# Four more blocks in three matmul passes, and a last chunk that is copied out between its transposes

## The chip, the cores and the metric

The kernel runs on one core of one Trainium2 chip. The metric is the device time of one execution in microseconds. A core has five engines that run their own instruction lists and wait for each other by semaphores: TensorE (PE; its weight loads are shown as PEld), VectorE (DVE), ScalarE (ACT), GpSimd (POOL) and SyncE (SP), which here only issues DMAs. All times in this document are microseconds unless ns is written.

## The reference

Two stages. The first is a polynomial attention with small sketches; the second is a mixture of four dense experts over its output `x` of 4352 tokens by 128 features, and it is where the change lies.

```python
p = domain_probs / (domain_probs.sum(-1, keepdims=True) + 1e-09)
out = np.zeros((N, D))                 # N = 4352, D = 128
for e in range(4):
    h = np.maximum(x @ w1[e], 0.0)     # w1[e]: 128 x 1024
    out += p[:, e:e + 1] * (h @ w2[e]) # w2[e]: 1024 x 128
```

Everything is float32.

## The kernel before

**Chunks and steps.** The 4352 tokens are cut into ten chunks, `CHUNKS = [128, 448, 480 x 7, 416]`, numbered 0 to 9. For each chunk `m` and each expert `e` the 1024 hidden features are eight blocks of 128. A step `i` does two blocks, so an expert takes four steps and a chunk sixteen (`NQ`); a half-step does one block. Tokens lie along the free axis, features on the partitions.

**First product of a block** (`first`, `third`, lines 1141, 1142, 1193): both operands are split beforehand into float32r parts, so that three matmul passes, `xa*wa`, `xb*wb` and `xd*wd`, replace one plain float32 product. Each pass is one instruction. Between the second and the third pass ScalarE scales the PSUM tile (line 1143).

**Second product of a block.** There are two forms. A *plain* block is evacuated by ScalarE into `hid` (line 1207) and multiplied with the float32 weight as one matmul, which the profile shows as two records (`o<-hid,w_sb`). A *three-pass* block is evacuated by ScalarE into `ha` (line 1197); VectorE makes `hb` from it (line 1169, in `lower`), and for each pair of blocks one `hd` (line 1172), or a single one where a block has no partner. Then three passes, `ha*va`, `hb*vb` and `hd*vd`, are issued (line 1274 in `passed`). The first two kinds accumulate in the PSUM tile `o0`, the `hd` passes and the plain products in `o1`.

**Which blocks are three-pass.** `THREE = (0, 1, 3, 4, 5, 6)` always; `OTHER = [2, 7]`. An `(m, e)` in `MORE_IN` also takes block 2, seven of eight; one in `ALL_IN` takes all eight. The extra weights are split while the kernel runs by `more_weight_parts(e, k)` at given steps: two ScalarE and two VectorE instructions of 128 columns per weight, in two parts.

**The order** of second products is written out by hand. A table (`DEAL`, `DEAL_MORE`, `DEAL_ALL`, `DEAL_END`) gives each product a slot, counted in half-steps from the expert's start; `to_due` queues them and `behind` issues those that are due between the first products. In `DEAL_MORE` the last `o1` product has slot 11, in `DEAL_ALL` slot 12 (`d7=12`), and block 7's `hb` product slot 10. `o0` and `o1` have one buffer each; the next expert's first `hd` products come at its slot 6.

**Closing an expert** (`close`, `gather`): after the last `o0` product ScalarE evacuates `o0` into `ev` (line 1277). After the last `o1` product, in chunks 7 to 9, ScalarE copies `o1` into `rest` (line 1358), and GpSimd adds both, multiplies with the gate and adds into `total` (lines 1361, 1368, 1370). In earlier chunks, and for expert 2 of chunk 9, VectorE adds `o1` (line 1355). `ev`, `rest` and `total` have one buffer, the gates two; SyncE reloads a gate when GpSimd is through with the older one.

**The end** (expert 3 of chunk 9, `at_end`): six blocks go in three passes. The last two, 2 and 7, are multiplied with the gate as they are evacuated (line 1203 on VectorE, 1209 on GpSimd) and go through `by_token`, where the tokens are the output's partitions: four products of up to 128 tokens for each block (line 1301) into one PSUM tile `y`, whose four column blocks hold 128, 128, 128 and 32 tokens. `finish` adds `ev`, `o1`, the gate and `total` on VectorE in six operations (lines 1285 to 1287). Four products with an identity (line 1308) then turn that sum and add it into `y`. ScalarE copies columns 0 and 1 to `rows` (line 1313), VectorE columns 2 and 3 (lines 1314, 1315), and four DMAs store one column block each (line 1318), two from SyncE's queue and two from ScalarE's.

Of the kernel before, what the change touches and what calls it, by code (L numbers as in the profile page):

```python
# [9 lines left out]
F32 = mybir.dt.float32  # L10
BF16 = mybir.dt.bfloat16
F32R = mybir.dt.float32r
# [6 lines left out]
def _ap(t, p0: int, np_: int, off: int, free):  # L19

    p = list(t.ap)[0]
    return bass.AP(t.tensor, t.offset + p0 * p[0] + off, [[p[0], np_]] + [list(d) for d in free])
# [3 lines left out]
def kernel(  # L26
# [24 lines left out]
    nc = tc.nc  # L51

    P = 128
    HP = 64
    B, H, S, D = q.shape
    E, DM, F = w1.shape
    R = 8
    R2 = 2 * R
    G = S // 32
# [6 lines left out]
    CW = 480  # L66
# [4 lines left out]
    OTHER = [b for b in range(FB) if b not in THREE]  # L71
# [18 lines left out]
        a0=4, b0=4, a1=4, b1=5, a2=5, a3=5, d0=6, d1=6, b2=6, a4=7, b3=7, a5=8, b4=8, d2=9, d3=9,  # L90
        b5=9, d4=10, d5=10, x6=11, x7=11,
    )
    ALL_IN = {(7, 2), (8, 2), (9, 2)}
    UNITS = [[P, 448, 512], [576, 512], [576, 512], [576, 512]]

    SPLITS = [
# [7 lines left out]

    CHUNKS = [P, 448] + [480] * 7 + [416]
    NC = len(CHUNKS)
    MORE_IN = {(2, 2), (3, 2), (4, 2), (5, 0), (5, 2), (5, 3), (6, 2), (7, 0), (7, 1), (7, 2), (7, 3), (8, 0), (8, 1), (8, 2), (8, 3), (9, 0), (9, 1), (9, 2)}
    MORE_AT = {0: (73, 75), 1: (56, 57), 2: (38, 39), 3: (77, 78)}
    START = [sum(CHUNKS[:m]) for m in range(NC)]
    assert all(sum(u) == S for u in UNITS) and sum(CHUNKS) == B * S  # L110
# [3 lines left out]
    apool = ctx.enter_context(tc.tile_pool(name="attn", bufs=1))  # L114
    mpool = ctx.enter_context(tc.tile_pool(name="moe", bufs=2))
# [5 lines left out]
    def psum(pool, tag):  # L121
        return pool.tile([P, 512], F32, tag=tag, name=tag)
# [63 lines left out]
    def more(m, e):  # L186
        return (m, e) in MORE_IN

    def three_of(m, e):
        return tuple(range(N3)) if at_end(m, e) else tuple(range(FB)) if (m, e) in ALL_IN else MORE if more(m, e) else THREE  # L190

    def deal_of(m, e):
        return DEAL_END if at_end(m, e) else DEAL_ALL if (m, e) in ALL_IN else DEAL_MORE if more(m, e) else DEAL

    def last_of(m, e, o):
        deal = deal_of(m, e)
        return max((p for p in deal if p[0] in ("ab" if o == 0 else "d" if at_end(m, e) else "dx")), key=lambda p: (deal[p], list(deal).index(p)))
# [4 lines left out]
    def second_weight(e, b):  # L202

        at = split_at(b)
        return w2_of[e, 0 if in_three(b) else 1][:, DM * at : DM * (at + 1)]
# [170 lines left out]
    def parts(m):  # L376

        c, end, at = START[m], START[m] + CHUNKS[m], 0
        while c < end:
            n = min(end, (c // S + 1) * S) - c  # L380
            yield c // S, c % S, n, at
            c, at = c + n, at + n
# [510 lines left out]
    def split(a, w, scale):  # L893
        nc.scalar.activation(a, w, ACTF.Copy, scale=scale * NEAR)

    def join(out, in0, scale, in1, op):
        nc.vector.scalar_tensor_tensor(out=out, in0=in0, scalar=scale, in1=in1, op0=ALU.mult, op1=op)
# [47 lines left out]
    def more_weight_parts(e, k=OTHER[0]):  # L945

        w = second_weight(e, k)
        if k != OTHER[0]:
            abd = apool.tile([P, 3 * P], F32R, tag="fs", name="vm")
            a, b, d = (abd[:, P * i : P * i + P] for i in range(3))  # L950
        elif e % 2 == 0:
            if "sr" not in more_home:
                more_home["sr"] = cpool.tile([P, 6 * P], F32R, tag="sr", name="vm")
            a, b, d = (more_home["sr"][:, P * i : P * i + P] for i in range(3 * (e // 2), 3 * (e // 2) + 3))
        else:
            ab = apool.tile([P, 2 * P], F32R, tag="kvz", bufs=2, name="vm")
            a, b = ab[:, 0:P], ab[:, P : 2 * P]
            d = (apool if e == 1 else cpool).tile([P, P], F32R, tag="rd" if e == 1 else "sq", name="vm")[:, :]
        split(a, w, 4096.0)
        join(b, w, 4096.0, a.bitcast(F32), ALU.subtract)  # L960
        yield
        split(a, w, 1.0)
        join(d, b.bitcast(F32), 1.0, a.bitcast(F32), ALU.subtract)
        w2_parts[e][k] = a, b, d
        yield
# [107 lines left out]
    def at_end(m, e):  # L1073
        return (m, e) == (NC - 1, E - 1)

    def block_of(m, e, k):
        return (THREE + tuple(OTHER))[k] if at_end(m, e) else k
# [180 lines left out]
    begun_o, evs = set(), {}  # L1258

    def passed(m, e, what, k, hd):  # L1260

        n, o = CHUNKS[m], 0 if what in "ab" else 1
        if what == "x" and at_end(m, e):
            return by_token(m, e, k, hd)
        if (m, e) not in acc:
            acc[m, e] = [None, None]
        if acc[m, e][o] is None:
            acc[m, e][o] = psum(ps_o, f"o{o}")
        first_one = (m, e, o) not in begun_o
        begun_o.add((m, e, o))  # L1270
        last = last_of(m, e, o) == what + str(k)
        b = block_of(m, e, k)
        w, h = (second_weight(e, b), hd) if what == "x" else (w2_parts[e][b]["abd".index(what)], hd["abd".index(what)])
        nc.tensor.matmul(acc[m, e][o][:, 0:n], w, h, start=first_one, stop=last)  # L1274
        if last and o == 0:
            evs[m, e] = mpool.tile([P, CW], F32, tag="ev", bufs=1, name="ev")
            nc.scalar.activation(evs[m, e][:, 0:n], acc[m, e][0][:, 0:n], ACTF.Copy, scale=1.0 + R12)
        if last and o == 1:
            finish(m, e) if at_end(m, e) else close(m, e)

    def finish(m, e):

        n, o1, ev, g = CHUNKS[m], acc.pop((m, e))[1], evs.pop((m, e)), gate.pop((m, e))
        for x in (slice(0, 2 * P), slice(2 * P, n)):
            nc.vector.tensor_tensor(out=ev[:, x], in0=ev[:, x], in1=o1[:, x], op=ALU.add)
            nc.vector.tensor_tensor(out=ev[:, x], in0=ev[:, x], in1=g[:, x], op=ALU.mult)
            nc.vector.tensor_tensor(out=ev[:, x], in0=ev[:, x], in1=total[m][:, x], op=ALU.add)
        last_sum[0] = ev
# [3 lines left out]
    def by_token(m, e, k, hd):  # L1292

        n = CHUNKS[m]
        if last_rows[0] is None:
            last_rows[0] = psum(ps_h, "h")
            last_rows.append(lpool.tile([P, 4 * P], F32, tag="kn", name="rows"))
        y, rows = last_rows
        cols = [(c, min(P, n - c)) for c in range(0, n, P)]
        for c, w in cols:  # L1300
            nc.tensor.matmul(  # L1301
                y[0:w, c : c + P], hd[:, c : c + w], second_weight(e, block_of(m, e, k)),
                start=(k == N3 and c == 0), stop=False, skip_group_check=True,
            )
        if k < FB - 1:
            return
        for c, w in cols:
            nc.tensor.matmul(
                y[0:w, c : c + P], last_sum[0][:, c : c + w], eye[0][:, :],
                start=False, stop=True, skip_group_check=True,  # L1310
            )
        ((b, at, _, _),) = parts(m)
        nc.scalar.copy(rows[:, 0 : 2 * P], y[:, 0 : 2 * P])
        nc.vector.tensor_copy(rows[:, 2 * P : 3 * P], y[:, 2 * P : 3 * P])
        nc.vector.tensor_copy(rows[0 : n - 3 * P, 3 * P :], y[0 : n - 3 * P, 3 * P :])
        for queue, c in ((nc.sync, 0), (nc.scalar, 2), (nc.sync, 1), (nc.scalar, 3)):
            c, w = cols[c]
            queue.dma_start(
                bass.AP(out.tensor, out.offset + (b * S + (at + c) // 32) * DM, [[DM, w // 32], [G * DM, 32], [1, DM]]),
                rows[0:w, c : c + P],  # L1320
            )

    eye = [None]
# [63 lines left out]
    def at_step(step, *calls):  # L1387
        to_part.setdefault(step, []).extend(calls)

    def next_of(parts_of):  # L1390
        return lambda: next(parts_of, None)
# [3 lines left out]
    for e, at in zip((2, 3, 0, 1), W2_AT):  # L1395
        parts_of = second_weight_parts(e)
        for hs in at:
            at_half.setdefault(hs, []).append(next_of(parts_of))
    for e, at in MORE_AT.items():
        parts_of = more_weight_parts(e)  # L1400
        for step in at:
            at_step(step, next_of(parts_of))
    parts_of = more_weight_parts(2, OTHER[1])
    for step in (113, 115):
        at_step(step, next_of(parts_of))
    for m in range(2, NC):
        tokens = token_parts(m)
        for step in (NQ * m - 4, NQ * m - 3):
# [6 lines left out]
    def close(m, e):  # L1415

        nonlocal ending
        ended = gather(m, e)
        next(ended)
        ending = chain(ending, ended)  # L1420
        closed[0] = m, e
# [38 lines left out]
    for i in range(len(steps) + LA):  # L1460
# [4 lines left out]
        if i < len(steps):  # L1465
            m, kq = steps[i]
# [72 lines left out]
```

## Time and profile before

| | us |
|---|---|
| median of 3 runs (lowest, highest) | 447.35 (447.32, 447.63) |
| the profiled execution's own time | 447.11 |
| its span, first to last instruction | 445.1 |
| TensorE busy | 437.4 (98%) |
| VectorE busy | 386.5 (87%) |
| ScalarE busy | 345.4 (78%) |
| GpSimd busy | 166.7 (37%) |

The profile is of one execution. A row of the timeline reads: start, duration, engine, line, operation, output and inputs by the program's names, shape, count, and in brackets the engine's idle time before it with what ended it. Matmul durations overlap, because they are pipelined. A row of a grouped view reads: count, busy us and mean ns, then idle time before the group. L1274 is line 1274 of the kernel before.

### The profile page before, as it was taken

To read this page: it belongs to the slowest core of one execution; us is meant where nothing else is said; L and a number is where in the kernel's file an instruction comes from. 1 tells how busy PE (TensorE), PEld (TensorE's weight loads), DVE (VectorE), ACT (ScalarE), POOL (GpSimd) and SP (SyncE) were. 2 spreads that over 40 slices of the span, in tenths; PEclk is the share of its full clock that TensorE was granted. 3 is DMA by queue.
4 is the path that set the end of the run, shared out by engine and by line. 5 is a ranking of instruction groups with operands and counts; after the bars stand their busy time and mean duration, and the time that the engine had idled before them with its cause. 6 is when DMAs were issued, how large, how long until landed. Compare 5 with 4: busy or idle time off the path is not lost.

```text
span 445.1 us, 8123 instructions
## 1 busy us (share of the span) xinstructions
PE 437.4 (98%) x2770; PEld 359.6 (81%) x2770; DVE 386.5 (87%) x616; ACT 345.4 (78%) x721; POOL 166.7 (37%) x243
## 2 busy tenths in 40 slices
PE   9999999999999999999999999999999999999994
PEld 6887678888887887778887888787888888889992
DVE  5998979978999789989997898889988998899893
ACT  4478898848888688868884888687888888888881
POOL 6358523212142023213351354133335463555451
PEclk9999999999999999999999999999999999999998
DMA  7945375224602430235114511260420012002100
GB/s 224 307 114 170 86 174 112 73 56 122 149 24 45 123 90 24 74 83 143 24 28 74 143 19 41 50 159 21 71 50 21 18 46 45 23 13 43 26 20 21
DMA packets 45525, 35.02 MB, mean 79 GB/s; under 512 B 21708, under 2 KB 40268, under 8 KB 45484
## 3 DMA queue, kind: packets, MB, share of 16 engines
q1 hardware_dynamic: 43960, 33.30, 30.0%
q0 software_dynamic: 1184, 1.05, 1.0%
q8 instruction: 22, 0.36, 0.3%
q10 hardware_dynamic: 340, 0.15, 0.2%
q14 instruction: 19, 0.16, 0.1%
HBM read 29.27 MB, written 5.21 MB: 77 GB/s over the span
## 4 chain that ended last, share of the span: by engine, by line
PE 92%; DMA 3%; DVE 1%; SPq 1%; ACT 1%; issue 1%; POOL 0%; DVEq 0%; ACTq 0%
PE o L1274 40%; PE h L1141 14%; PE h L1142 14%; PE h L1193 14%; PE h L272 6%; PE o L1253 3%; DMA w_sb<-in_moe_w_dram 2%; PE h L459 1%; PE o L272 1%; DMA dp<-in_moe_domain_probs_dram 1%; PE h L1301 1%; DVE hb L1169 0%; ACT h L1143 0%; SPq L178 0%; DMA s_raw<-in_S_dram 0%
## 5 line engine op out<-in xcount | busy, mean ns | idle before, releaser
L1143 ACT ACTIVATE h<-h 128x480 f32<-128x480 f32 (+2 forms) x288 | 158.9, 552 | 63.8 <-PE h L1142 56.5
L1169 DVE SCALAR_TENSOR_TENSOR hb<-h,ha 128x480 fp32r<-128x480 f32 (+2 forms) x225 | 140.5, 639 | 28.2 <-ACT ha L1197 25.8
L1172 DVE SCALAR_TENSOR_TENSOR hd<-ha,hb 128x960 fp32r<-128x960 f32 (+4 forms) x120 | 137.9, 1149 | 11.6 <-DVE hb L1169 0.5
L1141 PE MATMUL h<-xa,wa 128*128 128x480 f32 (+2 forms) x288 | 129.5, 450 | 0.0
L1197 ACT ACTIVATE ha<-h 128x480 fp32r<-128x480 f32 (+2 forms) x225 | 126.3, 561 | 0.1
L1193 PE MATMUL h<-xd,wd 128*128 128x480 f32 (+2 forms) x288 | 108.7, 377 | 0.1
L1142 PE MATMUL h<-xb,wb 128*128 128x480 f32 (+2 forms) x288 | 108.0, 375 | 0.0
L1368 POOL TENSOR_TENSOR ev<-ev,gate 128x256 f32<-128x256 f32 (+3 forms) x52 | 46.8, 900 | 146.1 <-DVE ev L1355 138.4
L1274 PE MATMUL o<-ha,vab 128*128 128x480 f32 (+2 forms) x204 | 76.7, 377 | 0.0
L1141 PEld LDWEIGHTS h<-xa,wa 128*128 128x128 f32 x288 | 54.2, 188 | 18.0 <-issue 11.4
L1142 PEld LDWEIGHTS h<-xb,wb 128*128 128x128 f32 x288 | 54.2, 188 | 17.5 <-issue 11.7
L1274 PE MATMUL o<-hd,vd 128*128 128x480 f32 (+2 forms) x204 | 63.7, 379 | 0.2 <-DVE hd L1172 0.2
L1193 PEld LDWEIGHTS h<-xd,wd 128*128 128x128 f32 x288 | 54.0, 188 | 8.9 <-ACT h L1143 0.8
L1370 POOL TENSOR_TENSOR total<-total,ev 128x256 f32<-128x256 f32 (+3 forms) x52 | 55.7, 1072 | 4.1
L1274 PE MATMUL o<-hb,vb 128*128 128x480 f32 (+2 forms) x136 | 51.2, 376 | 0.0
L1274 PE MATMUL o<-hid,w_sb 128*128 128x480 f32 (+2 forms) x90 | 43.2, 561 | 0.0
L1274 PEld LDWEIGHTS o<-hd,vd 128*128 128x128 f32 x204 | 37.8, 188 | 6.3 <-issue 0.8
L1274 PEld LDWEIGHTS o<-ha,vab 128*128 128x128 f32 x204 | 38.3, 188 | 5.1
L1361 POOL TENSOR_TENSOR ev<-ev,rest 128x256 f32<-128x256 f32 (+2 forms) x24 | 16.9, 726 | 63.3 <-ACT rest L1358 63.3
L1207 ACT ACTIVATE hid<-h 128x480 f32<-128x480 f32 (+2 forms) x62 | 34.7, 560 | 1.5 <-PE h L1193 1.4
L1368 POOL TENSOR_TENSOR total<-ev,gate 128x256 f32<-128x256 f32 (+3 forms) x18 | 15.8, 898 | 38.4 <-issue 23.0
L1274 PEld LDWEIGHTS o<-hb,vb 128*128 128x128 f32 x136 | 25.5, 188 | 4.0 <-DVE hb L1169 0.4
(166 smaller groups left out, 466.8 us busy)
## 6 DMA issues: line engine op xcount, KB each, us to landing
gate<-gates SPq DMA_DIRECT2D x16, 240.0 KB, 3.4
kn<-in_k_dram SPq DMA_DIRECT2D x4, 544.0 KB
vn<-in_v_dram SPq DMA_DIRECT2D x16, 128.0 KB, 5.9
qp<-qd SPq DMA_DIRECT2D x8, 256.0 KB
qp<-qd SPq DMA_DIRECT2D x6, 288.0 KB, 4.7
qb<-qd SPq DMA_DIRECT2D x6, 288.0 KB
qn<-in_q_dram SPq DMA_DIRECT2D x3, 544.0 KB
w_sb<-in_moe_w_dram SPq DMA_DIRECT2D x3, 512.0 KB
```

What stands on the lines that cost most here:

```text
L272: nc.tensor.matmul(out(s), weights(s), moving(s), **flags)
L1141: nc.tensor.matmul(g, wa[:, e, w], xa, start=True, stop=False)
L1142: nc.tensor.matmul(g, wb[:, e, w], xb, start=False, stop=True)
L1143: nc.scalar.activation(g, g, ACTF.Copy, scale=1.0 + R12)
L1169: nc.vector.scalar_tensor_tensor(out=hb, in0=g, scalar=0.0, in1=high, op0=ALU.max, op1=ALU.subtract)
L1172: nc.vector.scalar_tensor_tensor(out=d2, in0=a2.bitcast(F32), scalar=R12, in1=b2.bitcast(F32), op0=ALU.mult, op1=ALU.subtract)
L1193: nc.tensor.matmul(g, w, x, start=False, stop=True, skip_group_check=True)
L1197: nc.scalar.activation(ha, g, ACTF.Relu, scale=NEAR)
L1207: nc.scalar.activation(hid[i][j], g, ACTF.Relu)
L1274: nc.tensor.matmul(acc[m, e][o][:, 0:n], w, h, start=first_one, stop=last)
L1368: nc.gpsimd.tensor_tensor(out=to[:, x], in0=ev[:, x], in1=g[:, x], op=ALU.mult)
L1370: nc.gpsimd.tensor_tensor(out=total[m][:, x], in0=total[m][:, x], in1=ev[:, x], op=ALU.add)
```

## The change

Two things are edited.

1. *Second products.* Expert 1 of chunks 7, 8 and 9 moves from seven to eight three-pass blocks, and expert 0 of chunk 6 from six to seven. The weight of block 7 of expert 1 is therefore split too, at steps 114 and 115, into a tile that takes the place of `y` of the attention stage. The second half of the split of expert 2's block 7 moves from step 115 to step 117.
2. *The end.* The last expert's `o0` is evacuated into the buffer of `rest` instead of `ev`. The copies from PSUM are issued between the transposing products instead of behind them all, and the four stores take 32 partitions of all column blocks each, instead of all partitions of one column block. Run `g` of a partition group goes to every fourth output row group (`[4 * DM, t]`).

```diff
-    ALL_IN = {(7, 2), (8, 2), (9, 2)}
+    ALL_IN = {(7, 1), (7, 2), (8, 1), (8, 2), (9, 1), (9, 2)}
...
-    MORE_IN = {..., (5, 3), (6, 2), (7, 0), ...}
+    MORE_IN = {..., (5, 3), (6, 0), (6, 2), (7, 0), ...}
...  # more_weight_parts
-            abd = apool.tile([P, 3 * P], F32R, tag="fs", name="vm")
+            abd = apool.tile([P, 3 * P], F32R, tag="fs" if e == 2 else "y", name="vm")
...  # passed
-            evs[m, e] = mpool.tile([P, CW], F32, tag="ev", bufs=1, name="ev")
+            tag = "rest" if at_end(m, e) else "ev"
+            evs[m, e] = mpool.tile([P, CW], F32, tag=tag, bufs=1, name=tag)
             nc.scalar.activation(evs[m, e][:, 0:n], acc[m, e][0][:, 0:n], ACTF.Copy, scale=1.0 + R12)
...  # by_token
-        for c, w in cols:
+        ((b, at, _, _),) = parts(m)
+        for i, (c, w) in enumerate(cols):
             nc.tensor.matmul(
                 y[0:w, c : c + P], last_sum[0][:, c : c + w], eye[0][:, :],
                 start=False, stop=True, skip_group_check=True,
             )
-        ((b, at, _, _),) = parts(m)
-        nc.scalar.copy(rows[:, 0 : 2 * P], y[:, 0 : 2 * P])
-        nc.vector.tensor_copy(rows[:, 2 * P : 3 * P], y[:, 2 * P : 3 * P])
-        nc.vector.tensor_copy(rows[0 : n - 3 * P, 3 * P :], y[0 : n - 3 * P, 3 * P :])
-        for queue, c in ((nc.sync, 0), (nc.scalar, 2), (nc.sync, 1), (nc.scalar, 3)):
-            c, w = cols[c]
-            queue.dma_start(
-                bass.AP(out.tensor, out.offset + (b * S + (at + c) // 32) * DM, [[DM, w // 32], [G * DM, 32], [1, DM]]),
-                rows[0:w, c : c + P],
+            if i == 1:
+                nc.scalar.copy(rows[:, 0 : 2 * P], y[:, 0 : 2 * P])
+            elif i > 1:
+                nc.vector.tensor_copy(rows[0:w, c : c + P], y[0:w, c : c + P])
+        for g in range(4):
+            t = len([w for _, w in cols if w > 32 * g])
+            (nc.scalar if g % 2 else nc.sync).dma_start(
+                bass.AP(out.tensor, out.offset + (b * S + at // 32 + g) * DM, [[G * DM, 32], [4 * DM, t], [1, DM]]),
+                _ap(rows, 32 * g, 32, 0, [[P, t], [1, DM]]),
             )
...
-    parts_of = more_weight_parts(2, OTHER[1])
-    for step in (113, 115):
-        at_step(step, next_of(parts_of))
+    for e, at in ((2, (113, 117)), (1, (114, 115))):
+        parts_of = more_weight_parts(e, OTHER[1])
+        for step in at:
+            at_step(step, next_of(parts_of))
```

More of the change, by code (lines that the diff above doesn't have):

```diff
@@ L106 @@
     NC = len(CHUNKS)
-    MORE_IN = {(2, 2), (3, 2), (4, 2), (5, 0), (5, 2), (5, 3), (6, 2), (7, 0), (7, 1), (7, 2), (7, 3), (8, 0), (8, 1), (8, 2), (8, 3), (9, 0), (9, 1), (9, 2)}
+    MORE_IN = {(2, 2), (3, 2), (4, 2), (5, 0), (5, 2), (5, 3), (6, 0), (6, 2), (7, 0), (7, 1), (7, 2), (7, 3), (8, 0), (8, 1), (8, 2), (8, 3), (9, 0), (9, 1), (9, 2)}
     MORE_AT = {0: (73, 75), 1: (56, 57), 2: (38, 39), 3: (77, 78)}
```

## The prediction

> **What bounds the kernel now.** I read the page first, its span and its chain that ended last:
>
> ```profile
> span 445.1 us, 8123 instructions
> ...
> PE o L1274 40%; PE h L1141 14%; PE h L1142 14%; PE h L1193 14%; PE h L272 6%; PE o L1253 3%; DMA w_sb<-in_moe_w_dram 2%; PE h L459 1%; PE o L272 1%; DMA dp<-in_moe_domain_probs_dram 1%; PE h L1301 1%; DVE hb L1169 0%; ACT h L1143 0%; SPq L178 0%; DMA s_raw<-in_S_dram 0%
> ```
>
> The chain is TensorE's matmuls, first products and second products. The kernel is bound by the number of matmul passes, so taking passes away shortens it wherever TensorE does not come to wait. The profiled execution took 447.11 us, 2.0 more than its span, and the median of the runs is 447.35. I sum changes against the span of 445.1 and carry the difference over to the median unchanged.
>
> Next, the timeline of TensorE in the last fifth, at one plain second product (`hid,w_sb`):
>
> ```profile
> 304.19 0.97 PE L1274 MATMUL o<-hid,w_sb 128*128 128x480 f32 x2
> ...
> 305.22 0.38 PE L1142 MATMUL h<-xb,wb 128*128 128x480 f32 x1
> 305.44 0.38 PE L1193 MATMUL h<-xd,wd 128*128 128x480 f32 x1
> ```
>
> Durations overlap here, so starts must be read. One pass follows the other after 0.22 (305.22 to 305.44). Between 304.19 and 305.22 lie the plain product and one L1141 pass: 1.03 less 0.22 is 0.81 for the plain product. Three passes take 3 x 0.22 = 0.66. A converted block should thus give TensorE 0.15.
>
> Then whole experts, by windows from one expert's first `ha,vab` pass to the next one's (the columns are the window's length, and busy time with count of PE, PEld, DVE, ACT, POOL):
>
> ```profile
> 271.15:281.92 10.77, 10.77 (x48) 8.64 (x46) 9.39 (x14) 8.67 (x18) 4.17 (x4) 1.00 0.11 29
> 328.29:338.91 10.62, 10.62 (x49) 8.84 (x47) 8.67 (x12) 9.15 (x19) 3.62 (x4) 1.00 0.13 27
> 338.91:349.41 10.50, 10.50 (x50) 8.93 (x48) 9.52 (x13) 9.21 (x20) 5.84 (x6) 1.00 0.10 23
> 370.64:381.26 10.62, 10.62 (x48) 8.83 (x47) 8.68 (x12) 9.15 (x19) 3.61 (x4) 1.00 0.12 31
> 381.26:391.72 10.46, 10.46 (x50) 8.94 (x49) 9.47 (x13) 9.16 (x20) 5.84 (x6) 1.00 0.09 25
> 411.16:420.38 9.22, 9.22 (x49) 8.82 (x49) 7.79 (x12) 8.18 (x19) 3.19 (x4) 1.00 0.17 38
> 420.38:429.49 9.11, 9.11 (x49) 8.92 (x48) 8.26 (x13) 7.91 (x19) 5.17 (x6) 1.00 0.11 23
> ```
>
> The first row is expert 0 of chunk 6, with six blocks in three passes. Then come expert 1 (seven blocks) and expert 2 (all eight) of chunks 7, 8 and 9, in pairs. So the trace already holds the change for the neighbouring expert: all eight instead of seven is worth 0.12, 0.16 and 0.11. The granted clock is 1.00 in every row.
>
> **The second products.** Removed: four plain products, in (6,0), (7,1), (8,1), (9,1). Added: twelve passes. By the windows (7,1) and (8,1) give 0.12 and 0.16; (6,0), six to seven blocks at the same width, gives the 0.15 of the pass count. (9,1) would give 0.11, but I count it as nothing, for a reason in the next rows. Sum: 0.43 off TensorE.
>
> The price is on VectorE: ScalarE trades one activation for another, while each converted block adds a `hb` and half of a paired `hd`.
>
> ```profile
> L1169 DVE SCALAR_TENSOR_TENSOR hb<-h,ha 128x480 fp32r<-128x480 f32 x185 | 117.5, 649 | 22.3 <-ACT ha L1197 20.1 <-PE h L1142 1.9
> L1172 DVE SCALAR_TENSOR_TENSOR hd<-ha,hb 128x960 fp32r<-128x960 f32 x86 | 105.8, 1230 | 8.0 <-DVE hb L1169 0.5
> ...
> L1172 DVE SCALAR_TENSOR_TENSOR hd<-ha,hb 128x480 fp32r<-128x480 f32 x13 | 9.5, 730 | 1.7 <-PE h L1193 0.5
> ```
>
> For an ALL expert a single `hd` becomes a pair: 0.65 + (1.23 - 0.73) = 1.15 per block at most. In (6,0) it is 0.65 + 0.73, as a new single. Does VectorE have that room? Its timeline in expert 1 of chunk 7, the idle time in brackets:
>
> ```profile
> 335.88 0.66 DVE L1169 SCALAR_TENSOR_TENSOR hb<-h,ha 128x480 fp32r<-128x480 f32 x1 [0.55 <-PE h L1142]
> 336.96 0.66 DVE L1169 SCALAR_TENSOR_TENSOR hb<-h,ha 128x480 fp32r<-128x480 f32 x1 [0.42 <-ACT ha L1197]
> ...
> 340.02 0.66 DVE L1169 SCALAR_TENSOR_TENSOR hb<-h,ha 128x480 fp32r<-128x480 f32 x1 [0.57 <-ACT ha L1197]
> ```
>
> The new work falls just ahead of 335.88, and 0.55 + 0.42 + 0.57 = 1.54 of idle time follows before the busy expert 2 begins: 1.15 fits, with 0.39 left. What would be late next is a low product in expert 2, and that has room of its own:
>
> ```profile
> 344.54 1.22 DVE L1169 SCALAR_TENSOR_TENSOR hb<-h,ha 128x480 fp32r<-128x480 f32 x2
> ```
> ```profile
> 346.96 0.38 PE L1274 MATMUL o<-hb,vm 128*128 128x480 f32 x1
> ```
>
> Block 7's `hb` is done at 345.76 and used at 346.96, 1.20 later, so VectorE may lag by that much before TensorE waits. I price the cover at nothing lost; if it is gone, see the second rival. In chunk 9 it is different:
>
> ```profile
> 417.81 0.59 DVE L1169 SCALAR_TENSOR_TENSOR hb<-h,ha 128x416 fp32r<-128x416 f32 x1 [0.24 <-ACT ha L1197]
> 418.75 0.59 DVE L1169 SCALAR_TENSOR_TENSOR hb<-h,ha 128x416 fp32r<-128x416 f32 x1 [0.34 <-ACT ha L1197]
> ...
> 421.40 0.59 DVE L1169 SCALAR_TENSOR_TENSOR hb<-h,ha 128x416 fp32r<-128x416 f32 x1 [0.43 <-ACT ha L1197]
> ```
>
> Here the idle time is 1.01, about what the block adds (1.15 scaled by 416/480 is 1.00). After 421.40 VectorE shows no further idle time until 435.69, and TensorE's last second product waits for it (434.77, below). The tail belongs to VectorE, so TensorE's 0.11 in (9,1) is not passed on.
>
> The split of the weight (1,7) adds two ScalarE and two VectorE instructions at steps 114 and 115, 128 wide, each under the 0.73 of the 480-wide row; they and the second half of (2,7), moved from step 115 to 117, lie inside chunk 7's first expert and well before the use. The tile moves into the attention's `y`, free once its four DMAs have landed; nothing later writes it. A closing that comes one half-step later (last low product in slot 12 instead of 11) starts GpSimd's additions, and behind them SyncE's gate reload, later by an eighth of an expert, 1.3. GpSimd is busy 5.84 of 10.50 at the most in the windows, so I price this at nothing.
>
> **The end.** Its rows, from the timeline:
>
> ```profile
> 434.77 0.65 PE L1274 MATMUL o<-hd,vd 128*128 128x416 f32 x2 [0.19 <-DVE hd L1172]
> 435.13 0.52 ACT L1277 ACTIVATE ev<-o 128x416 f32<-128x416 f32 x1 [0.57 <-POOL total L1370]
> 435.27 2.47 PE L1301 MATMUL h<-w_sb,hid 128*128 128x128 f32 x16
> 435.69 0.42 DVE L1285 TENSOR_TENSOR ev<-ev,o 128x256 f32<-128x256 f32 x1 [0.47 <-ACT ev L1277]
> ...
> 437.67 1.27 PE L1308 MATMUL h<-eye,ev 128*128 128x128 f32 x8
> 438.98 0.37 ACT L1313 COPY rows<-h 128x256 f32<-128x256 f32 x1 [3.33 <-PE h L1308]
> 439.38 0.62 SPq L1318 DMA_DIRECT2D out_dram<-rows  x1
> 439.39 0.29 DVE L1314 COPY rows<-h 128x128 f32<-128x128 f32 x1 [1.42 <-ACT rows L1313]
> ...
> 439.71 0.66 ACTq L1318 DMA_DIRECT2D out_dram<-rows  x1
> ```
>
> `rest` instead of `ev`: ScalarE no longer waits 0.57 for GpSimd, and VectorE's six operations start some 0.2 earlier. That is worth nothing, because TensorE goes from 435.27 to 438.94 without a break.
>
> The copies between the matmuls: L1314 waited for L1313 although the two touch other columns, so two engines take turns at this one PSUM tile. In the changed program's order the third transposing product waits for ScalarE's copy, the fourth for VectorE's. The eight L1308 records take 1.27; the first four, columns 0 and 1, are through at about 438.38 (estimate: half of 1.27 and a little of the overlap). From there, with hand-overs of 0.04 as at 438.94 to 438.98: ScalarE's copy until 438.79, the third product (two records, about 0.45) until 439.3, VectorE's copy 0.29 until 439.62, the fourth product until 440.1, its copy until 440.45. All four DMAs wait for the whole of `rows` now, since each takes 32 partitions of every column block. The first issues fall at 440.48 instead of 439.38: 1.1 late. If the products did not wait, all would be ready about 439.2; that is the other bound.
>
> The DMAs themselves, from the views by line and of DMA issues:
>
> ```profile
> L1318 ACTq DMA_DIRECT2D out_dram<-rows x2: 462/561/660, 439.7 to 440.5; - x2
> DMA to landing us min/median/max: 3.5/3.5/3.5
> ```
> ```profile
> xd<-y SPq DMA_DIRECT2D x22, 64.0 KB, 1.7
> ...
> out_dram<-ob SPq DMA_DIRECT2D x16, 60.0 KB, 2.1
> ```
>
> The last one, 16 KB, is issued at 440.5 and lands 3.5 later, at 444.0; the span ends 1.1 after that. The new form (32 partitions, up to four runs of 512 bytes each) is the form of `xd<-y`, of the same 64 KB, which lands after 1.7; the other stores into the output, also of 32 partitions, take 2.1. The bounds are 1.7 and 3.5. I take 1.9, between the two like forms. The second issue of each queue follows the first by an issue time of 0.4 to 0.66, at about 441.0; landing at 442.9 instead of 444.0 takes 1.1 off the end, in spite of the later start.
>
> Sum: 0.43 + 1.1 = 1.53. Span 443.6, profiled execution 445.6, median 447.35 - 1.53 = 445.8.
>
> **The rivals.**
>
> *The new stores land no sooner.* For it: all are issued at once on two queues, and 3.5 is what this place shows. Against it: both rows of like form. Then the last landing is 441.0 + 3.5 = 444.5, 0.5 later; with 0.43 gained the result is about 447.4, no change. [...]
>
> *VectorE becomes the bound, slower than before.* The mechanism: idle time behind a wait for ScalarE is not room if the wait recurs after the inserted work. Then VectorE enters expert 2 by 1.15 late, and expert 2, where it is busy 9.5 of 10.5, adds to that. It decides from the point where the lag at block 7's `hb` passes 1.20; from there TensorE stops for the excess. With all 1.15 in excess in three chunks and 1.38 in (6,0) that is 4.8, less the 1.53: 450.6. Against it: the 1.54 of idle time, and that ScalarE's own arrivals do not move.
>
> *The products do not wait for the copies.* The stores start at about 439.2, 1.2 earlier than I say: 444.6. Against it stands the 1.42 wait.
>
> **How the numbers follow.** A change of 0.2%, 0.9 us, is about what a measurement of this kernel can tell from none. My forecast, 445.8, gets 0.74, of which 0.05 end with less than 0.9 gained (a landing past 2.5). The first rival, 447.4, gets 0.13; the second 0.08, mostly partial, a 0.01 of it within 0.2%; the third 0.05. Faster: 0.69 + 0.05 = 0.74. Same: 0.05 + 0.13 + 0.01 = 0.19. Slower: 0.07. The range takes the forecast's own (445.2, with landing after 1.7, the shortest issue, (9,1)'s 0.11 and a copy chain 0.2 shorter, to 446.8) and reaches to the first rival: 445.2 to 447.4.
>
> **What would show it.** Right: 41 plain second products instead of 45 at L1274; windows of 10.5 for expert 1 of chunks 7 and 8, with VectorE busy 9.5; ScalarE's last evacuation without its wait; the copies of the end alternating with the transposing products, first store issue near 440.5 less 0.4, and its landing under 2.1. Wrong: VectorE named as releaser of L1274 passes in chunks 7 to 9; stores landing after 3.5; or copies running beside the products.

## The result, and the profile after

| | before | after |
|---|---|---|
| median (lowest, highest), 6 runs each | 447.35 (447.32, 447.63) | 445.47 (445.19, 445.93) |
| the profiled execution's own time, its span | 447.11, 445.1 | 445.93, 443.9 |

The ratio is 0.9957, with a 95% interval of 0.9946 to 0.9969: 1.88 less, where 1.55 less was predicted. The gain is small, 0.4%, but the interval stays clear of 1. The profiled execution of after is the slowest of its six, so its span says less than its parts. The head of the page:

```profile
span 443.9 us, 8142 instructions
...
PE 437.3 (99%) x2774; PEld 360.1 (81%) x2774; DVE 391.5 (88%) x623; ACT 345.4 (78%) x723; POOL 169.6 (38%) x243
```

VectorE was busy 5.0 longer (386.5 before). TensorE did not stop for it in the four experts that changed. Their windows in after, each from its first `ha,vab` pass to the next expert's (columns as in the prediction):

```profile
272.03:282.64 10.61, 10.61 (x48) 8.82 (x47) 10.27 (x15) 8.65 (x17) 3.97 (x4) 1.00 0.11 26
329.01:339.46 10.45, 10.45 (x49) 9.01 (x48) 9.71 (x13) 9.06 (x20) 3.67 (x4) 1.00 0.14 29
...
371.18:381.65 10.47, 10.47 (x49) 9.01 (x48) 9.28 (x12) 8.89 (x19) 3.60 (x4) 1.00 0.12 31
...
411.59:420.68 9.09, 9.09 (x49) 8.90 (x49) 8.25 (x13) 7.91 (x19) 3.20 (x4) 1.00 0.17 38
```

The four are 10.61, 10.45, 10.47 and 9.09 long, against 10.77, 10.62, 10.62 and 9.22 before: 0.16, 0.17, 0.15 and 0.13 less, 0.61 together. That gain cannot be seen in the span, because this execution started late. The first row is of the timeline of before, the others of after:

```profile
28.11 0.47 PE L1141 MATMUL h<-xa,wa 128*128 128x448 f32 x1
```
```profile
20.76 0.77 PE L272 MATMUL h<-x_first,w_sb 128*64 128x128 f32 x8 [0.59 <-DMA w_sb<-in_moe_w_dram]
...
28.94 0.47 PE L1141 MATMUL h<-xa,wa 128*128 128x448 f32 x1
```

The first pass of the wide chunks is 0.83 late, mostly for a weight that had not landed (a wait of 0.59 that before does not have). The first by-token pass, at 435.58, is only 0.31 later than the 435.27 of before. Matched pass by pass, the lateness falls at just the four edited experts, from 0.88 to 0.31. A second profile of the changed kernel (run e_again) has its first wide pass at 28.32 and a span of 443.2, so the 0.83 is of one execution. Now the end in after:

```profile
434.93 0.52 ACT L1278 ACTIVATE rest<-o 128x416 f32<-128x416 f32 x1
...
435.58 2.47 PE L1302 MATMUL h<-w_sb,hid 128*128 128x128 f32 x16
...
437.98 0.71 PE L1310 MATMUL h<-eye,rest 128*128 128x128 f32 x4
438.73 0.37 ACT L1315 COPY rows<-h 128x256 f32<-128x256 f32 x1 [3.28 <-PE h L1310]
...
439.15 0.49 PE L1310 MATMUL h<-eye,rest 128*128 128x128 f32 x2 [0.46 <-ACT rows L1315]
439.68 0.29 DVE L1317 COPY rows<-h 128x128 f32<-128x128 f32 x1 [1.41 <-PE h L1310]
440.00 0.84 ACTq L1320 DMA_DIRECT2D out_dram<-rows  x2
...
440.02 0.41 PE L1310 MATMUL h<-eye,rest 128*32 128x128 f32 x2 [0.38 <-DVE rows L1317]
440.47 0.28 DVE L1317 COPY rows<-h 32x128 f32<-32x128 f32 x1 [0.50 <-PE h L1310]
440.81 0.82 SPq L1320 DMA_DIRECT2D out_dram<-rows  x2
```
```profile
L1320 SPq DMA_DIRECT2D out_dram<-rows x2: 337/384/432, 440.8 to 441.2; - x2
...
DMA to landing us min/median/max: 1.7/1.7/1.7
```

Product and copy alternate, each with the other named as its releaser: the staircase of the prediction. ScalarE's queue issues at 440.00, after the third block's copy, because its two stores need three column blocks only; SyncE's first store needs the fourth, and its second stands behind it. The last store, issued at 441.2, lands 1.7 later (3.5 before). From the first by-token pass to the span's end it is 443.9 - 435.58 = 8.3, before 445.1 - 435.27 = 9.8: the end gained 1.5.

What the stores do while in flight is in two stretches of each trace, the DMA engines' busy share and GB/s being the last columns (before, then after):

```profile
440.64:441.54 0.90, 0.00 (x0) 0.00 (x0) 0.00 (x0) 0.00 (x0) 0.00 (x0) 1.00 0.26 67
441.54:443.44 1.90, 0.00 (x0) 0.00 (x0) 0.00 (x0) 0.00 (x0) 0.00 (x0) 0.81 0.31 80
```
```profile
440.87:441.74 0.87, 0.00 (x0) 0.00 (x0) 0.00 (x0) 0.00 (x0) 0.00 (x0) 1.00 0.49 124
441.66:442.54 0.88, 0.00 (x0) 0.00 (x0) 0.00 (x0) 0.00 (x0) 0.00 (x0) 1.00 0.54 133
```

The old stores hold the share at 0.26 to 0.31 of 16 engines, which is four or five engines' worth, for 2.8; the new ones reach 0.5 and are through in two bursts of 0.9.

### The profile page after: what moved, and what is told of

Same layout as the page of the kernel before. It is cut to its first block, busy times and chain, and to the rows that moved or that the text cites. A ratio compares the mean times of both kernels' runs of the same rounds, so it can differ in the third digit from the quotient of the medians.

```text
span 443.9 us, 8142 instructions
## 1 busy us (share of the span) xinstructions
PE 437.3 (99%) x2774; PEld 360.1 (81%) x2774; DVE 391.5 (88%) x623; ACT 345.4 (78%) x723; POOL 169.6 (38%) x243
## 4 chain that ended last, share of the span: by engine, by line
PE 94%; DMA 3%; SPq 1%; DVE 1%; issue 0%; ACT 0%; POOL 0%; ACTq 0%
PE o L1274 41%; PE h L1193 14%; PE h L1141 14%; PE h L1142 14%; PE h L272 6%; PE o L1253 3%; DMA w_sb<-in_moe_w_dram 2%; PE h L459 1%; PE o L272 1%; SPq L178 1%; DMA dp<-in_moe_domain_probs_dram 1%; PE h L1302 1%; SPq L165 0%; DMA s_raw<-in_S_dram 0%; PE h L1310 0%
## 5 line engine op out<-in xcount | busy, mean ns | idle before, releaser
L1169 DVE SCALAR_TENSOR_TENSOR hb<-h,ha 128x480 fp32r<-128x480 f32 (+2 forms) x229 | 142.6, 638 | 22.4 <-ACT ha L1197 21.0
L1172 DVE SCALAR_TENSOR_TENSOR hd<-ha,hb 128x960 fp32r<-128x960 f32 (+3 forms) x121 | 140.7, 1163 | 11.7 <-DVE hb L1169 0.5
L1197 ACT ACTIVATE ha<-h 128x480 fp32r<-128x480 f32 (+2 forms) x229 | 128.5, 561 | 0.1
L1141 PE MATMUL h<-xa,wa 128*128 128x480 f32 (+2 forms) x288 | 128.0, 444 | 0.0
L1193 PE MATMUL h<-xd,wd 128*128 128x480 f32 (+2 forms) x288 | 108.8, 378 | 0.1
L1193 PEld LDWEIGHTS h<-xd,wd 128*128 128x128 f32 x288 | 54.1, 188 | 9.1 <-ACT h L1143 0.8
L1363 POOL TENSOR_TENSOR ev<-ev,rest 128x256 f32<-128x256 f32 (+2 forms) x24 | 19.4, 830 | 61.7 <-ACT rest L1360 61.7
L1274 PE MATMUL o<-hid,w_sb 128*128 128x480 f32 (+2 forms) x82 | 39.4, 562 | 0.0
L1207 ACT ACTIVATE hid<-h 128x480 f32<-128x480 f32 (+2 forms) x58 | 32.5, 561 | 1.5 <-PE h L1193 1.4
```

Source lines behind the costliest of these rows:

```text
L1141: nc.tensor.matmul(g, wa[:, e, w], xa, start=True, stop=False)
L1169: nc.vector.scalar_tensor_tensor(out=hb, in0=g, scalar=0.0, in1=high, op0=ALU.max, op1=ALU.subtract)
L1172: nc.vector.scalar_tensor_tensor(out=d2, in0=a2.bitcast(F32), scalar=R12, in1=b2.bitcast(F32), op0=ALU.mult, op1=ALU.subtract)
L1193: nc.tensor.matmul(g, w, x, start=False, stop=True, skip_group_check=True)
L1197: nc.scalar.activation(ha, g, ACTF.Relu, scale=NEAR)
L1207: nc.scalar.activation(hid[i][j], g, ACTF.Relu)
```

## The experiments

Runs sent together share a chip and the runs of the kernel before; each ratio is to those. At the end of this section a table sets the end of all kernels side by side.

**The two halves, each alone.** `e_second` is the kernel before with the `ALL_IN`, `MORE_IN`, `tag` and step edits; `e_end` is the kernel before with the edits in `passed` (`rest`) and `by_token`.

> The kernel before with the second products of the change alone; the end of the program stays as it was. Theory (TensorE passes): the traces show the four experts 0.12 to 0.17 shorter each, 0.57 together, so the time is 446.8 (447.35 - 0.55), with 41 plain products, and from the first by-token pass to the span's end still 9.8. Rival (the gain lies in the end alone, and the profiled run's late start of 0.83 hides a body that gained nothing): 447.3. Rival of VectorE (it becomes the bound): above 447.4.

> The kernel before with the end of the change alone: the tile of the last evacuation, the copies between the transposing products, the stores by 32 partitions. Theory: the end, counted from the first by-token pass to the span's end, is 8.3 instead of 9.8, so the time is 445.85 (447.35 - 1.5). The prediction had 446.25 (1.1 less). Rival (part of the 1.5 comes from the body): 446.3 or more.

Measured: `e_second` 446.65, ratio 0.9982 (0.9974 to 0.9991); `e_end` 445.8, ratio 0.9969 (0.9958 to 0.9981); before 447.46. In the traces the halves do not mix: the first by-token pass is at 434.67 in `e_second` (0.60 sooner than before) and at 435.24 in `e_end` (0.03 sooner), and from there the ends take 444.4 - 434.67 = 9.7 and 443.5 - 435.24 = 8.3. The rows of the first and then of the second:

```profile
span 444.4 us, 8140 instructions
```
```profile
434.67 2.47 PE L1301 MATMUL h<-w_sb,hid 128*128 128x128 f32 x16
```
```profile
span 443.5 us, 8125 instructions
```
```profile
435.24 2.47 PE L1302 MATMUL h<-w_sb,hid 128*128 128x128 f32 x16
```

So the second products give 0.6 and the end 1.5. The rival that the body (all that comes before the first by-token pass) gained nothing falls.

**Copies or stores?** `e_old_copies` is the changed kernel with all copies behind the products:

```diff
-            if i == 1:
-                nc.scalar.copy(rows[:, 0 : 2 * P], y[:, 0 : 2 * P])
-            elif i > 1:
-                nc.vector.tensor_copy(rows[0:w, c : c + P], y[0:w, c : c + P])
+        nc.scalar.copy(rows[:, 0 : 2 * P], y[:, 0 : 2 * P])
+        nc.vector.tensor_copy(rows[:, 2 * P : 3 * P], y[:, 2 * P : 3 * P])
+        nc.vector.tensor_copy(rows[0 : n - 3 * P, 3 * P :], y[0 : n - 3 * P, 3 * P :])
```

> The changed kernel with the three copies put back behind all four transposing products; stores of the new form. Theory (the stores' form is the whole gain, the new order of the copies costs time): the data is ready 4.6 after the first by-token pass instead of 5.2, and the last landing comes 0.6 sooner: end of 7.7, time 444.9. Rival (the order of the copies is a part of the gain): 446 or more, slower than the changed kernel's 445.47.

`e_old_stores` is the changed kernel with the old loop over `(nc.sync, 0), (nc.scalar, 2), (nc.sync, 1), (nc.scalar, 3)` in place of the loop over `g`.

> The changed kernel with the four old stores, by column block of up to 128 partitions; the copies stay between the products. Theory (stores' form): each store lands 3.5 after its issue; the last, of the fourth block, is issued about 5.2 after the first by-token pass and lands at 8.7 or later: end of 9.8, no better than before; time 446.8, the second products' gain alone. Rival (the gain is the order of the copies, or the earlier first stores): end of 8.3, 445.5.

Measured: `e_old_copies` 445.16, ratio 0.9949 (0.9937 to 0.9962); `e_old_stores` 445.86, ratio 0.9964 (0.9952 to 0.9976). The first has an end of 442.7 - 434.89 = 7.8, which is 0.45 shorter than with copies between the products (8.26 in e_again): by the traces the new order of the copies costs time, as predicted, and the stores' form earns more than the whole gain of the end. The medians of the two, 445.16 and 445.47, are too close to show it. The second was a miss: its end is 443.9 - 434.75 = 9.15, not 9.8. Its rows:

```profile
434.75 2.47 PE L1302 MATMUL h<-w_sb,hid 128*128 128x128 f32 x16
...
438.30 1.26 SPq L1320 DMA_DIRECT2D out_dram<-rows  x2
```
```profile
L1320 ACTq DMA_DIRECT2D out_dram<-rows x2: 517/589/661, 439.2 to 439.9; - x2
...
DMA to landing us min/median/max: 2.8/2.8/2.8
```

The last old store landed 2.8 after its issue, not 3.5. But 439.9 + 2.8 = 442.7 is 4.4 after the first issue at 438.30. In before that distance was 439.38 to 444.0, 4.6. The 3.5 was not the price of one store; the four together take some 4.5 from the first issue on. The early copy of blocks 0 and 1 therefore helps the old stores (first issue 3.55 after the first by-token pass instead of 4.1).

**Is it so?** `e_banks_old_stores` gives the by-token sums three PSUM tiles (below), which makes all data ready earlier but leaves the first issue where it is. The stores are the old ones.

> Three PSUM tiles as in the run before, with the old stores by column block. Theory (the old stores are held to a rate of their own: in three traces the last landing came 4.3 to 4.6 after the FIRST issue, whenever the last was issued): the first store leaves when it did with one tile, 3.55 after the first by-token pass, so the last landing is at 7.9 to 8.1 although all data is ready 1.1 sooner; end of 9.1, 0.8 over the changed kernel's 8.3, 0.8 slower than the changed kernel beside it. Rival (each old store lands some 3 after its own issue): last issue 4.5, landing 7.4, end of 8.5, like the changed kernel.

Measured 446.33, ratio 0.9977 (0.9969 to 0.9986); the changed kernel beside it 445.29.

```profile
L1321 SPq DMA_DIRECT2D out_dram<-rows x2: 575/599/623, 438.3 to 439.0; - x2
L1321 ACTq DMA_DIRECT2D out_dram<-rows x2: 639/644/650, 438.4 to 439.2; - x2
...
DMA to landing us min/median/max: 3.6/3.6/3.6
```

With the first by-token pass at 434.74, the last issue moved from 5.2 to 4.45 after it and the landing did not move (8.0). So the last store does not land at a fixed time after its own issue. The end of 9.4 is longer than the 9.1 expected: 1.4 instead of 1.1 lie behind the landing, and why stays open.

**Why are the old stores held to that rate?** `e_swapped` is `e_old_stores` with two dimensions of the destination exchanged, so that rows of the result lie in other places:

```diff
-                bass.AP(out.tensor, ..., [[DM, w // 32], [G * DM, 32], [1, DM]]),
+                bass.AP(out.tensor, ..., [[G * DM, 32], [DM, w // 32], [1, DM]]),
```

> The stores by column block of the kernel before (128 partitions each), with the two outer dimensions of the destination exchanged: 32 rows of one stride outside, 4 inside. Bytes, runs of 512 and the set of addresses are the same, but rows of the result change places. The copies are those of the changed kernel. Theory (what sped the stores up is the destination's outermost dimension, 32 instead of 4, over how many DMA engines the transfer is spread): the last store lands 1.7 to 2.1 after its issue at 5.2 past the first by-token pass, the end is 8.0 to 8.4, the time 444.7 to 445.1. Rival (what counts is 32 partitions instead of 128 for one transfer): as with the old stores, end of 9.15, time 445.9.

Measured 444.76, ratio 0.9939 (0.9926 to 0.9951).

```profile
L1320 ACTq DMA_DIRECT2D out_dram<-rows x2: 524/592/661, 439.3 to 440.0; - x2
...
DMA to landing us min/median/max: 1.6/1.6/1.6
```
```profile
439.65:440.65 1.00, 0.04 (x1) 0.00 (x0) 0.28 (x1) 0.00 (x0) 0.00 (x0) 1.00 0.48 143
```

Partitions, bytes, queues and issues are those of `e_old_stores`; the landing falls from 2.8 to 1.6 and the DMA share rises to 0.48 (0.29 to 0.32 in `e_old_stores`). What counts here is the destination's outer dimension, 32 or (for the three stores of 128 tokens) 4, not how many partitions a store takes. The exchanged form also writes four neighbouring rows in turn, but that is not needed: the rows of the new form are `4 * DM` apart, and its last store lands after 1.7. The share fits the theory that the outer dimension sets over how many DMA engines a store is spread: 0.29 to 0.32 is some five of the 16 engines' worth, and the exchanged form's 0.48 in the first 1.00 and 0.39 in the next 0.62 are six to eight. Which engines a single store takes, and by what rule, no run shows.

**Why do product and copy take turns?** `e_banks`:

```diff
-            last_rows[0] = psum(ps_h, "h")
+            last_rows[0] = [psum(ps_h, "h") for _ in range(3)]
...
+        of = {0: y[0][:, 0:P], P: y[0][:, P : 2 * P], 2 * P: y[1][:, 0:P], 3 * P: y[2][:, 0:P]}
```

with `of[c][0:w, :]` for `y[0:w, c : c + P]` in products and copies.

> The changed kernel with the by-token sums in three PSUM tiles (column blocks 0 and 1, block 2, block 3) instead of one, copies still between the products. Theory (engines take turns because they share the one PSUM tile): no product waits for a copy, the last copy is done 4.0 to 4.2 after the first by-token pass instead of 5.2, the last store is issued at 4.5 and lands at 6.2; end of 7.2, time 444.4. Rival (the waits come from something else, such as the tile rows or the bank's port): end as in the changed kernel, 8.3, time 445.5.

Measured 444.02, ratio 0.9923 (0.991 to 0.9935), the fastest kernel here.

```profile
434.62 2.47 PE L1303 MATMUL h<-w_sb,hid 128*128 128x128 f32 x16
...
437.03 1.27 PE L1311 MATMUL h<-eye,rest 128*128 128x128 f32 x8
437.77 0.37 ACT L1316 COPY rows<-h 128x256 f32<-128x256 f32 x1 [3.29 <-PE h L1311]
438.00 0.62 DVE L1318 COPY rows<-h 128x128 f32<-128x128 f32 x2 [0.69 <-PE h L1311]
438.37 0.84 ACTq L1321 DMA_DIRECT2D out_dram<-rows  x2
438.69 0.83 SPq L1321 DMA_DIRECT2D out_dram<-rows  x2
```

The eight product records run in 1.27 without a break while the first copies run beside them; the last copy is done 4.0 after the first by-token pass instead of 5.2, and the end takes 441.8 - 434.62 = 7.2. The turns came from the shared tile: TensorE's waits of 0.46 and 0.38 for a copy, there with one tile, are gone with three. What in the program or on the chip makes engines take turns at one tile, no run shows.

`e_order` issues the groups of `e_banks` as `for g in (1, 2, 3, 0)`.

> Three PSUM tiles with the new stores, issued in the order 1, 2, 3, 0, so that only the very last store (SyncE's second) waits for the fourth block's copy. Theory: both queues issue at 3.75 and 4.15 after the first by-token pass, the last landing is at 5.85 instead of 6.15, end of 6.9 instead of 7.2, time 443.7, 1.8 under the changed kernel. Rival (stores issued at once on both queues hold each other up): as with three tiles before, 444.0.

A miss: 444.83, ratio 0.9938 (0.9925 to 0.9951); the changed kernel beside it 445.29.

```profile
L1321 SPq DMA_DIRECT2D out_dram<-rows x2: 337/362/387, 438.7 to 439.1; - x2
L1321 ACTq DMA_DIRECT2D out_dram<-rows x2: 378/410/442, 438.7 to 439.1; - x2
DMA to landing us min/median/max: 2.0/2.0/2.0
```
```profile
439.60:440.75 1.15, 0.00 (x0) 0.00 (x0) 0.00 (x0) 0.00 (x0) 0.00 (x0) 1.00 0.77 182
```

The last issue came 0.3 sooner and the landing took 0.3 longer (2.0), with the stores of both queues in flight together and the engines 0.77 busy. So far the rival's mechanism holds: issuing sooner has stopped paying. Its time, 444.0, does not: the kernel took 0.8 more. The span ended 1.7 after this landing, against 1.0 in `e_banks`; that difference, nearly all of the 0.8, stays open.

**VectorE's room.** `e_dve2` does the last `hb` and `hd` of expert 1 twice in chunks 7 and 8:

```diff
-            nc.vector.scalar_tensor_tensor(out=hb, ...)
+            for _ in range(times):   # 2 for k == FB - 1 in (7, 1) and (8, 1), else 1
+                nc.vector.scalar_tensor_tensor(out=hb, ...)
```

and the same for `hd`.

> The changed kernel with VectorE's hb and hd of the last block of expert 1 done twice in chunks 7 and 8 (1.87 more of VectorE each, the same values again). In the changed kernel's trace VectorE has 0.16 of idle time left from that place through expert 2, and block 7's hb is ready 1.33 before its use. Theory (VectorE may lag by its idle time and this margin): it enters expert 2 late by 1.7, and TensorE stops for what passes the margin, 0.4 for each of the two chunks by hb, up to 1.4 by a hd that is used sooner: 446.3 to 448.3. Rival (VectorE's cover is far larger): 445.5. Rival (the waits for ScalarE recur behind it): 1.87 each, 449.2.

Measured 447.83, ratio 1.0011 (0.9999 to 1.0022): 2.4 above the changed kernel's 445.47, and the same by the two ratios; that is inside the expected band. TensorE's waits from 328 to 400, which are none in after, are here

```profile
PE o L1276 <- DVE hd L1174: 1.1, 2, 0.6
PE o L1276 <- DVE hb L1170: 0.2, 1, 0.2
```

and the two experts are 0.84 and 0.79 longer than in after:

```profile
328.33:339.62 11.29, 10.72 (x49) 8.94 (x48) 10.64 (x15) 9.19 (x20) 3.66 (x4) 1.00 0.14 28
...
371.76:383.02 11.26, 10.75 (x50) 8.94 (x49) 10.22 (x14) 9.03 (x19) 3.60 (x4) 1.00 0.12 29
```

Some 0.4 and 0.6 more are lost in expert 3 of the two chunks, by the starts of its passes. Of the 1.87 added in each chunk, 1.2 to 1.4 reached TensorE, so 0.5 to 0.7 of room was left after the change. The second rival is a real limit, and it lies that far away. The first wait is not where I had put it (block 7's `hb` in expert 2) but at the doubled `hd` itself.

**Two single points.** `e_ev` is the changed kernel with the last evacuation in `ev`; `e_no91` has `(9, 1)` taken out of `ALL_IN`; `e_again` is the changed kernel.

> The changed kernel with the last evacuation in the tile ev, as before, so that ScalarE waits for GpSimd. Theory (as predicted, worth nothing: TensorE has no break from the first by-token pass to the first copy): same time as the changed kernel beside it, 445.5, end of 8.3. Rival (the wait of 0.57 is a part of what the end gained): 446.1.

> The changed kernel with chunk 9's expert 1 at seven blocks again. The prediction counted that block as nothing, the tail being VectorE's; then the time stays 445.5. By the shift of TensorE's passes between the two traces (0.43 late before that expert, 0.31 after it) it is worth 0.12: 445.6, which the times can hardly tell, but the shift between this trace and the changed kernel's can.

> The changed kernel again, beside the next three on one chip: 445.5 (445.2 to 445.9 so far).

Measured: `e_ev` 445.28 (ratio 0.9955, 0.9943 to 0.9966) beside `e_again` 445.29 (0.9954, 0.9942 to 0.9965). ScalarE's wait is back and the time is the same:

```profile
434.69 0.52 ACT L1277 ACTIVATE ev<-o 128x416 f32<-128x416 f32 x1 [0.57 <-POOL total L1371]
```

`e_no91` was a miss: 446.2, ratio 0.9968 (0.9956 to 0.998), by the ratios 0.5 to 0.6 over the changed kernel (the intervals overlap), where 0 or 0.12 was expected. Its block itself is worth what the shift said: matched to before, TensorE's starts stay 0.28 to 0.31 early through chunk 9's expert 1, while in the kernels that keep the block they gain 0.11 to 0.13 there. But in the last expert `e_no91` loses 0.4. Its last `hd` passes, and then those of e_again:

```profile
434.88 0.64 PE L1274 MATMUL o<-hd,vd 128*128 128x416 f32 x2 [0.41 <-DVE hd L1172]
```
```profile
434.44 0.65 PE L1274 MATMUL o<-hd,vd 128*128 128x416 f32 x2 [0.20 <-DVE hd L1172]
```

VectorE had stood idle for 0.46 in expert 2, ahead of the `hd` at 424.60, behind a third pass of TensorE (`PE h L1193`); no such wait is in e_again. It enters the end late, TensorE waits for its last `hb` and 0.2 longer for its last `hd`, and the first by-token pass is at 435.38 instead of 434.94. So in the changed kernel this block is worth 0.44 up to there, not only its 0.12 of passes. Why VectorE has that wait in the kernel without the block stays open.

All ends, counted from the first by-token pass:

| kernel | copies | stores | first issue | last issue | landed | span's end |
|---|---|---|---|---|---|---|
| before | behind | old | 4.1 | 5.2 | 8.7 | 9.8 |
| e_old_stores | between | old | 3.55 | 5.2 | 8.0 | 9.15 |
| e_banks_old_stores | three tiles | old | 3.55 | 4.45 | 8.0 | 9.4 |
| e_swapped | between | old, exchanged | 3.55 | 5.2 | 6.8 | 7.9 |
| after | between | new | 4.4 | 5.6 | 7.3 | 8.3 |
| e_old_copies | behind | new | 4.4 | 5.1 | 6.8 | 7.8 |
| e_banks | three tiles | new | 3.75 | 4.45 | 6.2 | 7.2 |
| e_order | three tiles | new, other order | 3.75 | 4.15 | 6.1 | 7.8 |

## Why the prediction was right, and where it was off

The forecast of 445.8 against 445.47 was right in sign, and each of its two terms had the right mechanism; both were too small.

- *Second products, 0.43.* Measured 0.57 to 0.61 by windows and starts, 0.60 in `e_second`. (6,0), (7,1) and (8,1) gave 0.16, 0.17 and 0.15 for the 0.15, 0.12 and 0.16 forecast. The step that failed is "I count it as nothing", of (9,1): it gave 0.12. The reading behind it was right as far as it went, for the profile names no wait of VectorE in after from 412.62 to 435.52. But I set 1.01 of idle time against 1.00 of added work, from durations of single rows. The same two instructions on VectorE's timeline, before and after:

```profile
412.19 0.59 DVE L1169 SCALAR_TENSOR_TENSOR hb<-h,ha 128x416 fp32r<-128x416 f32 x1 [0.43 <-ACT ha L1197]
...
433.69 1.03 DVE L1172 SCALAR_TENSOR_TENSOR hd<-ha,hb 128x832 fp32r<-128x832 f32 x1
```
```profile
412.62 0.59 DVE L1169 SCALAR_TENSOR_TENSOR hb<-h,ha 128x416 fp32r<-128x416 f32 x1 [0.43 <-ACT ha L1197]
...
434.00 1.02 DVE L1172 SCALAR_TENSOR_TENSOR hd<-ha,hb 128x832 fp32r<-128x832 f32 x1
```

From the one to the other VectorE takes 21.50 and 21.38: the 1.01 of idle time is gone and 0.12 was gained, so only 0.89 was added, and the 0.12 that was left is what TensorE gained. Taken out of the changed kernel, the block costs more than this (`e_no91`).
- *VectorE's price hidden.* Right: no wait of TensorE for VectorE from 328 to 400. The margin left was forecast as 0.39 of idle time with up to 1.20 of lag; `e_dve2` found 0.5 to 0.7 in all, less than half of the 1.20 and the 0.39 together.
- *`rest` worth nothing.* Right, shown by `e_ev`. The weight's split and the moved tiles, too, left no trace in the starts of `e_second`, which change at the four experts alone.
- *Copies in a staircase.* Right: everything was ready 5.17 after the first by-token pass (440.75 - 435.58), forecast 5.18. The loss against copies behind the products is 0.45 in `e_old_copies`. What failed is "all four DMAs wait for the whole of `rows`": ScalarE's two need three column blocks and left 0.8 before SyncE's.
- *The stores.* Forecast: landed 7.6 after the first by-token pass (442.9 - 435.27), measured 7.3: the last issue 0.1 sooner, 1.7 instead of 1.9 for the landing. With 0.1 less behind the landing that makes the 0.4 by which 1.1 fell short of 1.5. The rival "no sooner" is out, and its price of 3.5 for one store was a misreading in the prediction too: it was the tail of the 4.6 that the four stores of before took from their first issue on; in `e_banks_old_stores`, where the last was issued 0.75 sooner than in `e_old_stores`, the landing stayed at 8.0.
- *The products do not wait.* Out for one PSUM tile; `e_banks` is what that rival described, and its end is 1.1 shorter, for the 1.2 between the rival's 444.6 and the forecast.

The parts of the trace give 0.57 + 1.5 = 2.1, the medians 1.88. In the profiles of the experiments TensorE reaches chunk 6 between 0.06 sooner and 0.27 later than in before's (0.88 later in the profiled run of after); the difference is of that size.

## What to carry to other kernels

Try for the stores at a kernel's end a larger outermost dimension of the destination: with 4 in three of four stores the last one landed 4.3 to 4.6 after the group's first issue, and the same bytes with 32 outermost landed 2.4 to 3.2 after it. A landing time read from one row can be that of a whole group (2.8 to 3.6 for the last old store, in four kernels), so measure it from the first issue of the group as well. And copies put between products gained here only where they read another PSUM tile than the products write: against copies behind the products on one tile they cost 0.45 with one tile and gained 0.6 with three.

## What was not expected of the hardware

The four old stores, 208 KB together, moved 67 to 85 GB/s (before, `e_old_stores`, `e_banks_old_stores`) whether the last was issued 4.45 or 5.2 after the first by-token pass. The new form moved 123 to 136 in the changed kernel (after, `e_again`), and 182 with both queues at once (`e_order`, 0.77 busy); there an issue 0.3 sooner bought nothing.
